# The seam between two matmul layers: loads of w1 and w2 issued ahead of the reload of x1, their conversions and splits moved behind the last tiles' relu

## The chip, the cores and the metric

One core of one Trainium2 chip runs the whole program. The metric is the device time of one execution in microseconds (us), as the median of several runs. TensorE (PE in the profile) does the matmuls, ScalarE (ACT) and VectorE (DVE) the elementwise work on its results, GpSimd (POOL) a part of it, and SyncE (SP) issues the transfers (DMA).

## The reference

A recurrence over time makes `attn_out`; its 3072 tokens of width 384 then go through two feed-forward layers. The seam between those two layers is what this document is about.

```python
def _moe_ref(x, w_in, w_out):            # layer 1: 3072 tokens, 384 -> 2048 -> 384
    h = x @ w_in
    relu6 = np.clip(h + 3.0, 0.0, 6.0)
    g = h * relu6 / 6.0
    return (g @ w_out)

def _moe2_ref(x, w1, w2, w3, w_out):     # layer 2: 384 -> 1024 (twice) -> 1024 -> 384
    a = x @ w1
    b = x @ w2
    h = a * b @ w3
    return (h @ w_out)
```

Everything is in float32 and the matmuls are made precise by splitting: each operand is kept as a high part and a low part, and one product is three matmuls (high by high, high by low, low by high).

## The kernel before

**Layer 1** runs in 6 blocks of 512 tokens (`j`), each in 16 tiles of 128 hidden units (`f`). For one tile `stage_a` does 9 matmuls into a PSUM tile `h` (three chunks of the inner dimension, three matmuls each). `relu_a` (ACT, L435) makes `t`, `evac_a` (DVE, L440) multiplies it with `h`, and `split_g` makes the high part `gh` (ACT, L447) and the low part `gl` (POOL, L451). `stage_b` does 9 matmuls of `gh` and `gl` with the output weights into the three PSUM tiles `acc`. It trails `stage_a` by two tiles (`LAG`), so the last tiles of the last block come on PE as: `h` of tile 14, `acc` of 12, `h` of 15, `acc` of 13, `acc` of 14, `acc` of 15. Then `evac_b` copies `acc` out (ACT, L464), and one DMA for each of the three stores the block to a scratch tensor `x1d` in device memory.

**Layer 2** has 6 blocks of 512 tokens and 8 tiles each. `load_x1` reads a block of `x1d` back into `x1r` (L582), `split_x1` makes `x1h` (ACT, L177) and `x1l` (L178; in block 0 on POOL for the first two of the three parts and on DVE for the third, by `XE`). `stage_c` does 18 matmuls with `x1h` and `x1l` and the weights of one tile (9 for w1 into `h`, 9 for w2 into a tile `wk`), `evac_c` multiplies the two, and `stage_d` multiplies that with the product of w3 and w_out. That product is computed in the kernel, by twelve matmuls at a time between the tiles of the last block of layer 1 (`w34_ticks`: the rows `wk<-wo2h,w3h`).

**The weights** arrive as packed halves and are put together on the chip. For one tile of w1 and w2: `load` issues a DMA of 768 KB into a staging buffer (`stage`, L151; three buffers `st` in turn, and one `stx` for tiles 3 and 7); `conv_a` (ACT, L166) writes `z` from it, into one of two buffers in turn; `conv_d` (DVE, L170) merges `z` into the staging buffer; `split` writes the high part (ACT, L177) and the low part (DVE, L178). The results are `w12ah` and `w12al` for tile 0, `w12h` and `w12l` for the others. `w12_ticks` is a generator that does this for the 8 tiles as a pipeline: tick `t` has `conv_a` of tile `t`, `split` of tile `t-2`, `conv_d` of tile `t-1` and the load of tile `t+2`.

**What sets the order.** There is no scheduler here: each engine takes its instructions in the order in which the code issues them, and waits at an instruction whose operands are not there. SP takes its DMA issues in the same way. Where the ticks stand between the tiles is written in the string `TK`: digit `2f` is the number of ticks of the running generator ahead of `relu_a` of tile `f` in the last block (only up to tile 13, `X1F`), digit `2f+1` the number behind `stage_b` in that step. Behind step 13 the kernel lets `w34_ticks` run out, closes its buffers, issues `load_x1(0)`, and starts `w12_ticks`. The buffer of `x1r` lies where the operands of the w3 product were, so `load_x1(0)` waits for the last of those matmuls.

Of the kernel before, what the change touches and what calls it, by code (L numbers as in the profile page):

```python
# [22 lines left out]
def kernel(  # L23
# [15 lines left out]
    nc = tc.nc  # L39
# [13 lines left out]
    KM = DM // 128  # L53
    KF = wio.shape[1] // (2 * DM)
# [49 lines left out]
    ZC = 2 * DM  # L104
    X1F = 13
    LO = 'w0 k0 r0 w1 k2 r1 w3 k1 n0 n3 r2 w2 k3 n1 r3 n2 s0'
    XE = 'ppv'
    XP = (14, 15, 15)
    XL = 13
    CMIN = 1e-18  # L110

    dram = ctx.enter_context(tc.tile_pool(name="dram", bufs=1, space=DRAM))
# [17 lines left out]
    def pst(tag):  # L130
        return ps.tile([128, 512], F32, tag=tag, name=tag, bufs={"h": 2, "acc": 3, "wk": 3}[tag])
# [7 lines left out]
    wp = wkv.enter_context(tc.tile_pool(name="wk_persist", bufs=1, side="right"))  # L139
    wt = wkv.enter_context(tc.tile_pool(name="wk_t", bufs=1, side="right"))  # L140


    PV = {'p': nc.gpsimd, 'v': nc.vector}

    def bits(ap):
        return ap.bitcast(U32)
# [1 line left out]
    def stage(src, x, n, buf=None):  # L148

        s = st_p.tile([128, 2 * ZC], U32, tag="st", name="st") if buf is None else buf  # L150
        nc.sync.dma_start(out=s[:, 0:2 * n].bitcast(U16), in_=src.bitcast(U16)[:, 4 * x * n + 1:4 * (x + 1) * n + 1])  # L151
        return s[:, 0:2 * n]
# [8 lines left out]
    def conv_a(st):  # L161
        w = st.rearrange("p (n two) -> p n two", two=2)[:, :, 0]
        half = st.bitcast(BF16).rearrange("p (n four) -> p n four", four=4)[:, :, 2]
        z = zs[zn[0] % NZ][:, 0:w.shape[1]]
        zn[0] += 1
        nc.scalar.activation(out=z.bitcast(FP16).rearrange("p (n two) -> p n two", two=2)[:, :, 1], in_=half, func=ACTF.Copy)  # L166
        return w, z

    def conv_d(w, z):
        nc.vector.scalar_tensor_tensor(w, w, 13, bits(z), op0=ALU.logical_shift_right, op1=ALU.bitwise_or)  # L170
        return w.bitcast(F32)
# [4 lines left out]
    def split(raw, hi, lo, lo_eng):  # L176
        nc.scalar.activation(out=hi, in_=raw, func=ACTF.Copy)  # L177
        lo_eng.tensor_tensor(lo, raw, hi.bitcast(F32), op=ALU.subtract)  # L178
# [295 lines left out]

    W0 = 1
    TT = 3
    TK = '11002010110100102302322303011101'
    AH = 4
    ML = 5

# [71 lines left out]
    def f2_open_x():  # L552
        F2.xctx = ExitStack()
        F2.xp = F2.xctx.enter_context(tc.tile_pool(name="x1", bufs=2, side="right", reuse_waits="tile"))

    def w12(f):
        return [t[:, f] for t in F2.w0] if f < W0 else [t[:, f - W0] for t in F2.w]

    def w12_ticks():

        st, zt = {}, {}

        def load(f):
            if f < KF2:
                st[f] = stage(w12d, f, ZC, F2.xp.tile([128, 2 * ZC], U32, tag="stx", name="stx", bufs=1) if f % 4 == 3 else None)

        load(0)
        load(1)
        for t in range(KF2 + 2):
            if t < KF2:  # L570
                zt[t] = conv_a(st[t])
            if t >= 2:
                split(zt.pop(t - 2), *w12(t - 2), nc.vector)
            if 1 <= t < KF2 + 1:
                zt[t - 1] = conv_d(*zt[t - 1])
                st.pop(t - 1)
            load(t + 2)
            yield

    def load_x1(j):  # L580
        s = F2.xp.tile([128, KM, N2], F32, tag="x1r", name="x1r")
        nc.sync.dma_start(out=s, in_=x1d[:, :, j * N2:(j + 1) * N2])  # L582
        F2.x1[j] = [s, F2.xp.tile([128, KM, N2], F32R, tag="x1h", name="x1h"),
                    F2.xp.tile([128, KM, N2], F32R, tag="x1l", name="x1l")]

    def split_x1(j, m):
        s, xh, xl = F2.x1[j]
        split(s[:, m], xh[:, m], xl[:, m], PV[XE[m]] if j == 0 else nc.gpsimd)

    def stage_c(j, f):  # L590
        _, xh, xl = F2.x1[j]
# [216 lines left out]
    if True:  # L808
        make_identity(nc, ident)
        nc.gpsimd.memset(ones, 1.0)  # L810
        for z in zs:
            nc.gpsimd.memset(z, 0.0)
        for x in LO.split()[0:LO1]:
            LD[x[0]](int(x[1]))
        nc.sync.dma_start(out=ubk[0:G], in_=uT)
        nc.scalar.activation(out=ones, in_=ones, func=ACTF.Copy)
        nc.gpsimd.memset(Dp, 0.0)
        nc.gpsimd.memset(Df, 0.0)
        for t in Wb:
            nc.gpsimd.memset(t[0:G, PAD - 1:PAD], 0.0)  # L820
        for t in St:
            nc.gpsimd.memset(t, 0.0)
        for x in LO.split()[LO1:]:
            LD[x[0]](int(x[1]))
        nc.sync.dma_start(out=ubc, in_=u.rearrange("h d -> (h d)").unsqueeze(0).to_broadcast([128, DM]))
        pw = pst("h")

        def warm():
            i16 = ident.bitcast(BF16)
            nc.tensor.matmul(pw[:, 0:256], i16[:, 0:128], i16, start=True, stop=True)  # L830

        wl = w34_ticks()
        units = {}
        nf = dict.fromkeys("GEMHLBV", 0)
        FF = {"G": stage_a, "E": relu_a, "M": evac_a, "H": lambda j, f: split_g(1, j, f, 0),
              "L": lambda j, f: split_g(1, j, f, 1), "B": stage_b, "V": evac_b}
        ONE = {"S": w_load, "O": wio_open, "a": w_a, "d": w_d, "i": w_i, "p": w_p, "D": warm, "w": lambda: next(wl)}

        for x in " ".join(ORDER).split():
            if len(x) > 1:  # L840
                uu = int(x[1:])
                if uu not in units:
                    units[uu] = unit(uu)
                units[uu][x[0]]()
            elif x in nf:
                FF[x](*divmod(nf[x], KM if x == "V" else KF))
                nf[x] += 1
            else:
                ONE[x]()

        steps = [(1, j, f) for j in range(NB) for f in range(KF)] + [(2, j, f) for j in range(NB2) for f in range(KF2)]
        last = NB - 1
        for si in range(last * KF, len(steps) + LAG):
            ph, j, f = steps[si] if si < len(steps) else (3, 0, 0)
            if ph == 1:
                stage_a(j, f)
                if j == last:
                    if f == 0:
                        wkv.close()
                        xt0.close()  # L860
                        w34_open()
                    if f <= X1F:
                        for _ in range(int(TK[2 * f])):
                            next(wl, None)
                relu_a(j, f)
                evac_a(j, f)
                split_g(ph, j, f)
            if ph == 2:
                stage_c(j, f)
                if j == 0:  # L870
                    next(wl, None)
                    split(W34.r[:, f], W34.h[:, f], W34.l[:, f], nc.vector)
                evac_c(j, f)
                split_g(ph, j, f)
            if si >= LAG:
                b = steps[si - LAG]
                if not (ph == 2 and b[0] == 1):
                    (stage_b if b[0] == 1 else stage_d)(*b[1:])
                    if b[0] == 1 and b[2] == KF - 1:
                        for m in range(KM):  # L880
                            evac_b(b[1], m)
            if (ph, j) == (1, last):
                if f == X1F:
                    for _ in wl:
                        pass
                    W34.tctx.close()
                    f2_open_x()
                    load_x1(0)
                    wl = w12_ticks()
                for _ in range(int(TK[2 * f + 1])):  # L890
                    next(wl, None)
                for m in range(KM):
                    if f == XP[m]:
                        split_x1(0, m)
                if f == KF - 1:
                    ph1.close()
                    f2_open_w()
                    for x in range(LAG):
                        stage_b(*steps[si - LAG + 1 + x][1:])
                    for m in range(KM):  # L900
                        evac_b(last, m)
                    next(wl, None)
            if ph == 2:
                if j in (2, 3, 4) and f % 2 == 0:
                    guard_w((j - 2) * 4 + f // 2)
                if (j, f) == (5, 0):
                    guard()
                if f == 1 and j + 1 < NB2:
                    load_x1(j + 1)
                if f in (4, 5, 6) and j + 1 < NB2:  # L910
                    split_x1(j + 1, f - 4)
        man.close()
        F2.xctx.close()
        F2.wctx.close()
        W34.ctx.close()
        main.close()
        okv = nc.values_load(flag, min_val=0, max_val=1)
# [70 lines left out]
```

## Time and profile of the kernel before

| what | value |
|---|---|
| median of 3 runs | 887.28 us (886.37 to 887.92) |
| the profiled execution's own time | 888.7 us |
| its span, first to last instruction | 887.0 us |
| mean granted clock of TensorE | 0.994 of full speed |
| PE busy in the span | 98% |
| ACT, DVE, POOL busy in the span | 37%, 40%, 42% |

A line of the timeline reads: start in us, duration in us, engine, line of the kernel, operation, tile written, tile read, shape, and in square brackets how long the engine was idle before it and what ended that. `acc<-gh,wio2h` is a matmul that writes `acc` with `gh` streaming and a piece of `wio2h` as the stationary weights. A window row has, for each engine, busy us and the number of instructions, then the granted clock of TensorE (1.00 is 2.4 GHz, 0.50 is 1.2 GHz), the busy share of the DMA engines and the GB/s moved. Tile numbers are not in the rows: of the last block, the row order tells them.

### The profile page before, as it was taken

The numbers are of one execution on the slowest core, as the hardware profiler recorded it, in microseconds if no ns is written. First come the engines' busy times: TensorE is split into PE (matmuls) and PEld (weight loads), VectorE is DVE, ScalarE is ACT, GpSimd is POOL, SyncE is SP. The second block draws the span as 40 slices with busy tenths as digits, with TensorE's granted clock in tenths as the row PEclk, the third lists the DMA queues.
The fourth block names the chain that finished last, engine by engine and source line by source line (L and its number), as shares of the span: only waits on it lengthen the run. The fifth ranks groups of instructions, "written<-read, shape, count | busy, mean of one in ns | idle before, by whom it ended". The sixth has DMA issues, their size and how long they took to land.

```text
span 887.0 us, 13899 instructions
## 1 busy us (share of the span) xinstructions
PE 865.2 (98%) x5752; PEld 707.5 (80%) x5752; DVE 357.5 (40%) x537; ACT 330.5 (37%) x556; POOL 375.8 (42%) x337
## 2 busy tenths in 40 slices
PE   7999999999999999999999999899999999999997
PEld 6777677888888888888888888688888888888785
DVE  7799884444444444444213444155111111212110
ACT  1666633333333333343335555365222222222211
POOL 6677877464555555455232211224232222323221
PEclk9999999999999999999999999999999999999999
DMA  9756541212322122221203452560110404030001
GB/s 257 240 193 229 179 123 46 62 62 62 97 62 75 59 86 66 83 81 53 65 1 108 136 176 85 178 212 2 48 45 1 154 1 155 1 133 1 36 1 39
DMA packets 29239, 81.92 MB, mean 92 GB/s; under 512 B 3312, under 2 KB 3440, under 8 KB 29168
## 3 DMA queue, kind: packets, MB, share of 16 engines
q1 hardware_dynamic: 29168, 80.95, 27.9%
q8 instruction: 47, 0.77, 0.3%
q14 instruction: 24, 0.20, 0.1%
HBM read 71.50 MB, written 9.44 MB: 91 GB/s over the span
## 4 chain that ended last, share of the span: by engine, by line
PE 78%; issue 12%; POOL 5%; DVE 3%; ACT 1%; DMA 0%; SPq 0%; POOLq 0%; ACTq 0%; DVEq 0%
PE h L182 9%; PE acc L183 9%; PE acc L182 9%; PE acc L184 9%; PE h L184 9%; PE h L183 9%; PE wk L369 5%; PE wk L183 4%; PE wk L184 4%; PE wk L182 4%; POOL gl L451 4%; PE wk L304 3%; PE wk L348 1%; PE wk L292 1%; POOL A L315 1%
## 5 line engine op out<-in xcount | busy, mean ns | idle before, releaser
L451 POOL TENSOR_TENSOR gl<-t,gh 128x512 fp32r<-128x512 f32 x144 | 192.0, 1334 | 390.6 <-ACT gh L447 390.5
L447 ACT ACTIVATE gh<-t 128x512 fp32r<-128x512 f32 x144 | 91.0, 632 | 193.1 <-DVE t L606 105.9
L440 DVE SCALAR_TENSOR_TENSOR t<-t,h 128x512 f32<-128x512 f32 x96 | 65.3, 681 | 136.2 <-ACT t L435 135.8
L606 DVE TENSOR_TENSOR t<-t,wk 128x512 f32<-128x512 f32 x48 | 33.0, 687 | 202.9 <-PE wk L184 202.9
L435 ACT ACTIVATE t<-h 128x512 f32<-128x512 f32 x96 | 57.3, 597 | 136.8 <-PE h L184 125.1
L182 PE MATMUL h<-xh,wioh 128*128 128x512 f32 x234 | 94.9, 406 | 0.3 <-DVE t L440 0.3
L182 PE MATMUL acc<-gh,wioh 128*128 128x512 f32 x234 | 93.1, 398 | 0.0
L183 PE MATMUL acc<-gl,wioh 128*128 128x512 f32 x234 | 91.6, 392 | 1.0 <-POOL gl L451 1.0
L184 PE MATMUL h<-xh,wiol 128*128 128x512 f32 x234 | 92.2, 394 | 0.3 <-DVE wiol L802 0.3
L183 PE MATMUL h<-xl,wioh 128*128 128x512 f32 x234 | 91.7, 392 | 0.0
L184 PE MATMUL acc<-gh,wiol 128*128 128x512 f32 x234 | 91.4, 391 | 0.0
L605 ACT ACTIVATE t<-h 128x512 f32<-128x512 f32 x48 | 28.6, 596 | 99.6 <-PE h L184 99.6
L183 PE MATMUL acc<-gl,w34h 128*128 128x512 f32 x144 | 56.3, 391 | 0.0
L184 PE MATMUL acc<-gh,w34l 128*128 128x512 f32 x144 | 56.3, 391 | 0.0
L182 PE MATMUL acc<-gh,w34h 128*128 128x512 f32 x144 | 56.2, 390 | 0.0
L182 PEld LDWEIGHTS h<-xh,wioh 128*128 128x128 f32 x234 | 44.0, 188 | 11.7 <-issue 1.3
L184 PEld LDWEIGHTS h<-xh,wiol 128*128 128x128 f32 x234 | 43.9, 188 | 11.1 <-DVE wiol L802 1.3
L183 PEld LDWEIGHTS acc<-gl,wioh 128*128 128x128 f32 x234 | 44.0, 188 | 10.5 <-POOL gl L451 1.6
L184 PEld LDWEIGHTS acc<-gh,wiol 128*128 128x128 f32 x234 | 43.9, 188 | 9.5
L182 PEld LDWEIGHTS acc<-gh,wioh 128*128 128x128 f32 x234 | 44.0, 188 | 9.4 <-issue 0.2
L166 ACT ACTIVATE z<-st 128x768 f16<-128x768 bf16 (+2 forms) x46 | 41.2, 902 | 27.0 <-DVE st L170 8.5
L183 PEld LDWEIGHTS h<-xl,wioh 128*128 128x128 f32 x234 | 44.0, 188 | 8.5
(141 smaller groups left out, 1727.0 us busy)
## 6 DMA issues: line engine op xcount, KB each, us to landing
nat<-in_rkv_dram SPq DMA_DIRECT2D x20, 640.0 KB, 3.9
st<-in_wio_dram SPq DMA_DIRECT2D x16, 768.0 KB, 4.7
st<-in_w3T_dram SPq DMA_DIRECT2D x16, 512.0 KB, 4.4
W<-in_wT_dram SPq DMA_DIRECT2D x24, 224.0 KB, 2.7
K<-in_kT_dram SPq DMA_DIRECT2D x24, 224.0 KB, 2.6
R<-in_rT_dram SPq DMA_DIRECT2D x24, 224.0 KB, 3.0
st<-in_wT_dram SPq DMA_DIRECT2D x12, 448.0 KB, 6.0
x1d<-ev SPq DMA_DIRECT2D x18, 256.0 KB, 2.9
```

The lines of the kernel that those rows point to most:

```text
L166: nc.scalar.activation(out=z.bitcast(FP16).rearrange("p (n two) -> p n two", two=2)[:, :, 1], in_=half, func=ACTF.Copy)
L182: nc.tensor.matmul(ps_ap, lh, rh, start=first, stop=False)
L183: nc.tensor.matmul(ps_ap, lh, rl, start=False, stop=False)
L184: nc.tensor.matmul(ps_ap, ll, rh, start=False, stop=last)
L304: nc.tensor.matmul(d["sc"][h2][:, pr * C:(pr + 1) * C], kh[sl, pr, :], rh[sl, pr, :], start=(pr == 0), stop=(pr == NP - 1), skip_group_che ...
L369: nc.tensor.matmul(px[32 * j:32 * j + 32, m * C:(m + 1) * C], lhs, rhs, start=j not in seen, stop=False, skip_group_check=True)
L435: nc.scalar.activation(out=t, in_=hp[:, 0:N1], func=ACTF.Relu, bias=3.0)
L440: nc.vector.scalar_tensor_tensor(t, t, 6.0, hp[:, 0:N1], op0=ALU.min, op1=ALU.mult)
L447: nc.scalar.activation(out=gh, in_=t, func=ACTF.Copy)
L451: nc.gpsimd.tensor_tensor(gl, t, gh.bitcast(F32), op=ALU.subtract)
L605: nc.scalar.activation(out=a, in_=pp[0][:, 0:N2], func=ACTF.Copy)
L606: nc.vector.tensor_tensor(a, a, pp[1][:, 0:N2], op=ALU.mult)
```

## The change

Four edits, all at the seam:

1. `w12_ticks` issues three loads (tiles 0, 1, 2) at its start instead of two, and stops there once; the loads of the first three tiles are issued ahead of `load_x1(0)` instead of behind it. The number of loads is the same.
2. `TK` holds no tick behind step 13 and two behind step 14: `conv_a` of tiles 0 and 1 now both stand behind relu and split of tile 14.
3. In a tick, `split` of tile `t-2` now stands ahead of `conv_a` of tile `t`.
4. The three parts of `split_x1(0)` are all issued behind step 15, all three low parts on DVE; the tick with `split` of tile 0 and `conv_a` of tile 2 follows them.

```diff
-    XE = 'ppv'
-    XP = (14, 15, 15)
-    XL = 13
...
-    TK = '11002010110100102102322303011101'
+    TK = '11002010110100102302322303000200'
...
-        load(0)
-        load(1)
+        for f in range(3):
+            load(f)
+        yield
         for t in range(KF2 + 2):
+            if t >= 2:
+                split(zt.pop(t - 2), *w12(t - 2), nc.vector)
             if t < KF2:
                 zt[t] = conv_a(st[t])
-            if t >= 2:
-                split(zt.pop(t - 2), *w12(t - 2), nc.vector)
             if 1 <= t < KF2 + 1:
                 zt[t - 1] = conv_d(*zt[t - 1])
                 st.pop(t - 1)
-            load(t + 2)
+            if t >= 1:
+                load(t + 2)
             yield
...
-        split(s[:, m], xh[:, m], xl[:, m], PV[XE[m]] if j == 0 else nc.gpsimd)
+        split(s[:, m], xh[:, m], xl[:, m], nc.vector if j == 0 else nc.gpsimd)
...
                     f2_open_x()
+                    wl = w12_ticks()
+                    next(wl)
                     load_x1(0)
-                    wl = w12_ticks()
                 for _ in range(int(TK[2 * f + 1])):
                     next(wl, None)
-                for m in range(KM):
-                    if f == XP[m]:
+                if f == KF - 1:
+                    for m in range(KM):
                         split_x1(0, m)
-                if f == KF - 1:
+                    next(wl)
                     ph1.close()
                     f2_open_w()
```

On ACT, from the last copy of the w3 product to the first copy of `acc`, before (`t` is the relu of layer 1, the numbers are buffers; `h_5323` and `h_5355` are tiles 14 and 15):

```order
L523 ACTIVATE w34_4550<-wk_5256 128x384
L166 ACTIVATE z0_72<-st_5316 128x768
L435 ACTIVATE t_5333<-h_5323 128x512
L447 ACTIVATE gh_5336<-t_5333 128x512
L166 ACTIVATE z1_73<-st_5318 128x768
L177 ACTIVATE x1h_5314<-x1r_5312 128x512
L435 ACTIVATE t_5365<-h_5355 128x512
L447 ACTIVATE gh_5368<-t_5365 128x512
L166 ACTIVATE z0_72<-st_5321 128x768
L177 ACTIVATE w12ah_4551<-st_5316 128x768
L177 ACTIVATE x1h_5314<-x1r_5312 128x512 x2
L464 ACTIVATE ev_5419<-acc_4647 128x512
```

And in the changed kernel (`h_5322` and `h_5353` are tiles 14 and 15):

```order
L518 ACTIVATE w34_4550<-wk_5256 128x384
L430 ACTIVATE t_5332<-h_5322 128x512
L442 ACTIVATE gh_5335<-t_5332 128x512
L161 ACTIVATE z0_72<-st_5312 128x768
L161 ACTIVATE z1_73<-st_5314 128x768
L430 ACTIVATE t_5363<-h_5353 128x512
L442 ACTIVATE gh_5366<-t_5363 128x512
L172 ACTIVATE x1h_5320<-x1r_5318 128x512 x3
L172 ACTIVATE w12ah_4551<-st_5312 128x768
L161 ACTIVATE z0_72<-st_5316 128x768
L459 ACTIVATE ev_5419<-acc_4647 128x512
```

The conversion of tile 0 moved from ahead of the relu of tile 14 to behind it, and all that touches x1 moved behind the relu of tile 15.

On SP, from the last load of w3 on, before:

```order
L151 DMA st2_5078<-in_w3T_dram 128x2048 [waits DMAHW4_49,DVE_49]
L582 DMA x1r_5312<-x1d_57 128x3x512 [waits PE_49]
L151 DMA st_5316<-in_w12_dram 128x3072 [waits DMAHW3_49]
L151 DMA st_5318<-in_w12_dram 128x3072 [waits DMAHW5_49,DVE_49]
L151 DMA st_5321<-in_w12_dram 128x3072 [waits DMAHW7_49,DVE_49]
L151 DMA stx_5351<-in_w12_dram 128x3072 [waits DVE_49]
```

And in the changed kernel:

```order
L146 DMA st2_5078<-in_w3T_dram 128x2048 [waits DMAHW4_49,DVE_49]
L146 DMA st_5312<-in_w12_dram 128x3072 [waits DMAHW3_49]
L146 DMA st_5314<-in_w12_dram 128x3072 [waits DMAHW5_49,DVE_49]
L146 DMA st_5316<-in_w12_dram 128x3072 [waits DMAHW7_49,DVE_49]
L579 DMA x1r_5318<-x1d_57 128x3x512 [waits PE_49]
L146 DMA stx_5351<-in_w12_dram 128x3072 [waits DVE_49]
```

The issue that waits for PE (`x1r`) stood ahead of the three loads into `st` and now stands behind them.

On DVE, from the evacuation of tile 14 on (`t<-t,h`), before:

```order
L440 SCALAR_TENSOR_TENSOR t_5333<-t_5333,h_5323 128x512
L170 SCALAR_TENSOR_TENSOR st_5316<-st_5316,z0_72 128x768
L440 SCALAR_TENSOR_TENSOR t_5365<-t_5365,h_5355 128x512
L178 TENSOR_TENSOR w12al_4552<-st_5316,w12ah_4551 128x768
L170 SCALAR_TENSOR_TENSOR st_5318<-st_5318,z1_73 128x768
L178 TENSOR_TENSOR x1l_5315<-x1r_5312,x1h_5314 128x512
L178 TENSOR_TENSOR w12l_5400<-st_5318,w12h_5399 128x768
```

And in the changed kernel:

```order
L435 SCALAR_TENSOR_TENSOR t_5332<-t_5332,h_5322 128x512
L165 SCALAR_TENSOR_TENSOR st_5312<-st_5312,z0_72 128x768
L435 SCALAR_TENSOR_TENSOR t_5363<-t_5363,h_5353 128x512
L173 TENSOR_TENSOR x1l_5321<-x1r_5318,x1h_5320 128x512 x3
L173 TENSOR_TENSOR w12al_4552<-st_5312,w12ah_4551 128x768
L165 SCALAR_TENSOR_TENSOR st_5314<-st_5314,z1_73 128x768
L173 TENSOR_TENSOR w12l_5400<-st_5314,w12h_5399 128x768
```

DVE now does all three low parts of x1, ahead of the low part of tile 0's weights; POOL has two subtractions less.

## Rows read from the trace of the kernel before

**Rows 1.** The page's first part: engine, busy us, share of span, instructions.

```profile
PE 865.2 (98%) x5752; PEld 707.5 (80%) x5752; DVE 357.5 (40%) x537; ACT 330.5 (37%) x556; POOL 375.8 (42%) x337
```

**Rows 2.** Timeline of PE, end of layer 1: ends of h 14, h 15, acc 13; then acc 14 and on.

```profile
562.71 0.39 PE L184 MATMUL h<-xh,wio2l 128*128 128x512 f32 x1
...
566.79 0.39 PE L184 MATMUL h<-xh,wio2l 128*128 128x512 f32 x1
...
568.83 0.39 PE L184 MATMUL acc<-gh,wio2l 128*128 128x512 f32 x1
572.82 0.79 PE L182 MATMUL acc<-gh,wio2h 128*128 128x512 f32 x1 [3.61 <-ACT gh L447]
574.18 0.79 PE L183 MATMUL acc<-gl,wio2h 128*128 128x512 f32 x1 [0.57 <-POOL gl L451]
...
580.51 0.39 PE L182 MATMUL h<-x1h,w12ah 128*128 128x512 f32 x1
```

**Rows 3.** Windows of the same stretch, all engines.

```profile
569.10:572.80 3.70, 0.12 (x1) 0.00 (x0) 1.38 (x2) 2.16 (x4) 0.00 (x0) 0.95 1.02 425
572.80:579.00 6.20, 5.61 (x12) 4.09 (x13) 2.03 (x4) 5.28 (x8) 4.47 (x4) 0.50 0.20 84
```

**Rows 4.** Timeline of ACT: relu and gh of tile 13, then from tile 14 on.

```profile
556.98 0.60 ACT L435 ACTIVATE t<-h 128x512 f32<-128x512 f32 x1 [2.85 <-PE h L184]
558.33 0.63 ACT L447 ACTIVATE gh<-t 128x512 fp32r<-128x512 f32 x1 [0.75 <-DVE t L440]
...
569.89 1.06 ACT L166 ACTIVATE z<-st 128x768 f16<-128x768 bf16 x1 [8.33 <-DMA st<-in_w_dram]
570.82 0.57 ACT L435 ACTIVATE t<-h 128x512 f32<-128x512 f32 x1
...
576.91 0.89 ACT L177 ACTIVATE w12ah<-st 128x768 fp32r<-128x768 f32 x1
577.70 1.14 ACT L177 ACTIVATE x1h<-x1r 128x512 fp32r<-128x512 f32 x2
```

**Rows 5.** Windows of PE alone, behind the seam.

```profile
580.51:622.00 41.49, 41.49 (x181) 1.00 0.32 112
```

**Rows 6.** Timeline of SP: the reload of x1, then the loads of w1 and w2.

```profile
561.07 0.63 SPq L582 DMA_DIRECT2D x1r<-x1d  x1
561.75 2.48 SPq L151 DMA_DIRECT2D st<-in_w_dram  x3
```

**Rows 7.** What SP waited for, 530 to 620 us (total, times, longest).

```profile
SPq L582 <- PE wk L184: 18.3, 1, 18.3
```

**Rows 8.** DMA issues 560.5 to 565 us: count, KB each, median us to landing.

```profile
st<-in_w_dram SPq DMA_DIRECT2D x3, 768.0 KB, 8.4
x1r<-x1d SPq DMA_DIRECT2D x1, 768.0 KB, 6.5
stx<-in_w_dram SPq DMA_DIRECT2D x1, 768.0 KB, 11.2
```

**Rows 9.** Timeline of DVE: last low parts of w3, conversion of tile 0.

```profile
550.63 0.69 DVE L178 TENSOR_TENSOR w3l<-st,w3h 128x512 fp32r<-128x512 f32 x1 [0.79 <-ACT w3h L177]
...
553.78 1.33 DVE L178 TENSOR_TENSOR w3l<-st,w3h 128x512 fp32r<-128x512 f32 x1 [1.26 <-ACT w3h L177]
...
572.02 0.95 DVE L170 SCALAR_TENSOR_TENSOR st<-st,z 128x768 uint32<-128x768 uint32 x1
```

**Rows 10.** Timeline of POOL: gl of tiles 12 and 13.

```profile
553.27 1.30 POOL L451 TENSOR_TENSOR gl<-t,gh 128x512 fp32r<-128x512 f32 x1 [7.64 <-ACT gh L447]
559.04 1.29 POOL L451 TENSOR_TENSOR gl<-t,gh 128x512 fp32r<-128x512 f32 x1 [4.47 <-ACT gh L447]
```

**Rows 11.** Windows: a stretch with little DMA, and one with a short wait of PE.

```profile
540.00:560.00 20.00, 19.39 (x98) 17.29 (x98) 8.39 (x12) 9.60 (x17) 3.57 (x3) 1.00 0.09 27
100.00:102.00 2.00, 1.98 (x8) 1.43 (x8) 0.65 (x2) 1.87 (x3) 2.00 (x2) 1.00 1.04 368
```

**Rows 12.** Timeline of PE in that second stretch.

```profile
100.03 0.50 PE L183 MATMUL acc<-gl,wioh 128*128 128x512 f32 x1 [0.97 <-POOL gl L451]
```

More of the change, by code (lines that the diff above doesn't have):

```diff
@@ L140 @@
     wt = wkv.enter_context(tc.tile_pool(name="wk_t", bufs=1, side="right"))
-    PV = {'p': nc.gpsimd, 'v': nc.vector}
     def bits(ap):
@@ L476 @@
     TT = 3
-    TK = '11002010110100102302322303011101'
+    TK = '11002010110100102302322303000200'
     AH = 4
```

## The prediction

> **What bounds the kernel now.** The page's first part comes first: PE is busy for 98% of the span [rows 1], so only a stretch in which PE waits, or runs at a lower clock, can give anything. The list of PE's waits has two of them at the seam and none behind it, which the PE timeline shows in place [rows 2] and a window confirms: from 580.51 to 622 us PE is busy for 41.49 of 41.49 us [rows 5]. At the seam the last matmul of acc of tile 13 starts at 568.83; the first of tile 14 starts at 572.82, after an idle time of 3.61 us that ended with gh; the second waits once more for gl. The windows show what follows: granted clock 0.95 while PE idles and 0.50 (the level of 1.2 GHz) from 572.8 to 579.0 [rows 3].
>
> Next, why gh was late. The matmuls of h of tile 14 end at 562.71 + 0.39 = 563.10 [rows 2], yet its relu starts at 570.82 [rows 4]. Ahead of it in ACT's queue stands the conversion of tile 0 of w1 and w2, which sat from 561.6 to 569.89 waiting for its DMA, 8.33 us [rows 4]. And why that DMA was late: SP waited 18.3 us for the last matmul of the w3 product before it could issue the reload of x1 [rows 7], at 561.07, and the loads stood behind it, from 561.75 on [rows 6]. So a wait of SP for PE made ACT wait, and ACT made PE wait.
>
> **What the seam costs.** Nine matmuls take 568.83 - 566.79 = 2.04 us at full clock [rows 2], 0.227 each. Without waits acc of tile 14 would start at 568.83 + 0.23 = 569.06, and the 18 matmuls of tiles 14 and 15 would end 4.09 us later: layer 2 would start at 573.15. It starts at 580.51 [rows 2]. The seam costs **7.36 us**: 3.76 ahead of the first matmul, 1.13 between first and second (1.36 instead of 0.23), and 2.47 because the other 17 take 6.33 instead of 3.86, at the lower clock.
>
> **Relu of tile 14 (edit 2).** The conversion leaves the place ahead of it. For tile 13 the relu started at 556.98, gh ended at 558.96 and gl at 560.33 [rows 4, 10], so the chain from relu to gl takes 3.35 us and to gh 1.98. By the same lag relu 14 starts near 563.20, gh is there at 565.2 and gl at 566.55, while PE wants them at 569.06: 2.5 us to spare. This removes the 7.36, if nothing new is late.
>
> **Conversions of tiles 0 and 1 (edits 1 and 2).** They now stand between gh 14 and relu 15: two of 1.06 us [rows 4], from 565.1 to 567.2. h 15 ends at 567.18 [rows 2], so they just fit. Then gh 15 is there at 569.3 and gl 15 at 570.6; PE wants gl 15 at 569.06 + 2.04 + 0.23 = 571.33. Spare: 0.7 us. The cover is the h and acc matmuls of tiles 15 and 13; every tenth beyond 0.7 by which the conversions end late would be paid in full.
>
> **The loads (edit 1).** The three loads no longer stand behind the issue that waits for PE; what they wait for is their buffers, the last of which is free when the low part of w3 that starts at 550.63 ends, 551.3 [rows 9]. In the old queue loads took from 8.1 us (the conversion's start, 569.89, less the issue) to 11.2 us to land [rows 4, 6, 8]; even 11.2 would give 562.5, ahead of 565.1. The DMA engines are 9% busy from 540 to 560 [rows 11], so I take nothing for them. The last loads of w3 stand ahead of them in the queue; at most they lose the difference between 8.4 and 6.5, 1.9 us [rows 8], and the last low part of w3 is there at 553.78 + 1.33 = 555.11 [rows 9], 6 us ahead of the end of the product that reads it, 561.07 [rows 6, 7]. Nothing is charged for that either.
>
> **The reload of x1.** Still issued at 561.07, with one transfer behind it instead of four. It took 6.5 us then [rows 8]; 567.6 is ahead of 569.2, when ACT has done gh 15.
>
> **The splits (edits 3 and 4).** On ACT: three high parts of x1 at 0.54 apart (two took 1.14), then w12ah, 0.89 [rows 4]: 569.2 + 1.62 + 0.89 = 571.7, ahead of 573.15. On DVE there is a catch. A subtraction with both inputs in SBUF that started at 553.78, while POOL worked on gl from 553.27 to 554.57, took 1.33 us and ended 0.54 behind POOL's end, where one without POOL beside it took 0.69 [rows 9, 10]. Here the first low part of x1 meets gl 15, which holds until 570.6. So it ends at 571.15, the other two at about 572.4, and w12al, at the 0.95 us that the conversion of as many columns takes [rows 9], at **573.3**. The third matmul of layer 2 is the first that reads w12al, at 573.15 + 0.45 = 573.6, its weight load a matmul earlier, 573.4. It fits by 0.1: I charge 0, with 0.4 as the upper bound.
>
> The Trainium skill (SBUF — State Buffer, Who interferes with whom) says that a VectorE instruction with two SBUF inputs and a GpSimd instruction that reads SBUF exclude each other for the whole instruction, so that the later one blocks fully. The row at 553.78 agrees. By that rule moving work from POOL to DVE gains nothing beside gl 15, which speaks against edit 4; by the sum above it still fits.
>
> **Tile 1 and on.** conv_d of tile 1 ends at 574.2, beside the copies of acc (the last needs the matmuls up to 573.3 and ends near 574.1); w12h of tile 1 at 575.1, w12l at 576.1. PE wants them at 573.15 + 18 x 0.227 = 577.2. Spare 1.1. The load of tile 4 waits for the end of w12al, 573.3; were it as slow as 6.5, it is there at 579.8, and PE wants tile 4 some 14 us later. From there on every engine has the time per tile that it had, and PE had no wait there [rows 5], so all that PE gains at the seam reaches the end.
>
> **Sum.** -7.36 us, between -7.4 and -5.9. The profiled execution took 888.7 with its 887.0 of span, so it would take 881.3 (span 879.6). It lies 1.4 above the median of 887.28; the same taken off the median gives **879.9 us**.
>
> **Rivals.**
> *A small wait stays at the seam.* If conversion 1 ends half a microsecond or a whole one later than I reckon, relu 15, gl 15, then the low parts of x1 (which wait for gl 15) and w12al each slip by that. For it: the spare there is 0.1. Against: the queues ahead are idle, so nothing shows what should delay it. PE would wait 0.4 to 1.5 us. At 100.03 a wait of 0.97 us left the clock at 1.00 [rows 11, 12], so it costs no more than itself: about 880.9.
> *The loads don't run ahead.* If SP got to them only at 561.07, they would take the first places in the queue and x1 the fourth. x1 would land as the fourth did, two microseconds ahead of the fifth's 564.27 + 11.2 = 575.5 [rows 6, 8], at 573.5; its high parts and w12ah end 2.5 us later, 576.0, and PE, having waited about as long as before, pays the 2.47 for the clock: 578.5, a gain of 2.0, 885.3. Against it: in the order the first load carries no wait for PE.
> *x1 late enough to cost more than the old wait.* The mechanism is the fourth place in one queue. Layer 2 starts 2.5 us behind the landing of x1, plus 2.47 for the clock, so the seam is longer than before once x1 lands later than 580.51 - 4.97 = 575.5, where the fifth transfer landed. One more place, 577.5, gives +2.0: 889.3. Against it: only stx is in the queue with it.
> The Trainium skill (DMA: Bandwidth & Descriptors, Queues, rings and completion order) says that each DMA engine takes the descriptors of a ring in order, and the landing times, 6.5 us for the first and 11.2 for the last of five issued within 3.2 us, agree. By that rule x1 now pays for whatever of the three loads is left; by the dates above nothing is left.
> *The change doesn't do what it says,* and ACT still reaches relu 14 behind a wait: 887.3. The order on ACT speaks against it.
>
> **How the numbers follow.** Forecast (gain of 6.9 to 7.5) 0.78; small wait 0.14; loads not ahead 0.03; x1 late 0.02; no effect 0.03. The range runs from the lowest run of before less 7.4, 878.9, to the small wait at its largest (gain 5.9, 881.4) plus the 0.6 by which the highest run lies over the median and a little for the clock: 882.4. A measurement of this kernel can tell about 0.2%, 1.8 us, from no change. The case of the loads not ahead lies on that line and is put down as 0.02 faster and 0.01 not. Faster by more than that: 0.78 + 0.14 + 0.02 = 0.94; within it 0.01 + 0.03 = 0.04; slower 0.02.
>
> **What would show it.** In the changed trace: the first load of tile 0 issued before 552 and x1 still at 561; ACT's relu of tile 14 near 563.2 with no DMA wait ahead of it; PE without an idle row from 554 to 622; layer 2's first matmul near 573.15; a granted clock of 1.00 in every window of the seam; the first low part of x1 on DVE stretched to about 1.4 us by gl 15. Wrong would be: an idle row of PE at acc of tile 15 (conversions late), at the first matmul with x1 (reload late) or with w12al (DVE late), or a clock of 0.50 anywhere behind 560.

## The result, and the profile after

The changed kernel takes 881.01 us, median of 4 runs (878.82 to 881.93), against 887.39 (886.37 to 887.92) for the kernel before beside it: ratio 0.9919, 95% interval 0.9899 to 0.994. A second timing with more runs gave 881.05 (879.56 to 883.16) against 888.45, the same ratio 0.9919, interval 0.9904 to 0.9935. The ratios are not the quotients of the two medians, which are 0.9928 and 0.9917. So the change saves 6.4 us by the first pair of medians, 7.4 by the second, and 7.2 by the ratio; the forecast was 7.4, to 879.9, in a range of 878.9 to 882.4.

The page's first line of the changed kernel (engine, busy us, share of span, instructions; before: [rows 1]):

```profile
PE 860.0 (98%) x5752; PEld 704.2 (80%) x5752; DVE 359.7 (41%) x539; ACT 331.0 (38%) x556; POOL 373.7 (43%) x335
```

PE is busy for 5.2 us less, with the same number of matmuls. Idle time that goes does not show there; matmuls that no longer run at the lower clock do. Of the 5.2, the seam has 3.2 (27.7 us busy before, 24.5 now, between the two ends given below); the rest lies ahead of the seam, and the second trace of the changed kernel does not have it (862.2 in all, 3.0 less). DVE has two instructions more and POOL two less, the low parts of x1. The span is 878.7 us.

The PE timeline of the changed kernel at the seam (first matmuls of acc of tile 14, acc of tile 15, layer 2, and the first that reads w12al; before: [rows 2]):

```profile
568.47 0.39 PE L177 MATMUL acc<-gh,wio2h 128*128 128x512 f32 x1
...
570.51 0.39 PE L177 MATMUL acc<-gh,wio2h 128*128 128x512 f32 x1
...
572.56 0.39 PE L177 MATMUL h<-x1h,w12ah 128*128 128x512 f32 x1
...
573.01 0.39 PE L179 MATMUL h<-x1h,w12al 128*128 128x512 f32 x1
```

No row has a wait in brackets. The same stretch in windows (us, then busy us and count of PE, PEld, DVE, ACT, POOL, the granted clock, DMA share, GB/s; before: [rows 3]):

```profile
560.00:566.00 6.00, 6.00 (x29) 5.00 (x28) 1.08 (x2) 3.13 (x5) 1.30 (x1) 1.00 0.67 186
566.00:572.00 6.00, 6.00 (x28) 4.99 (x27) 4.25 (x6) 5.07 (x9) 1.30 (x1) 1.00 0.19 79
572.00:578.00 6.00, 6.00 (x28) 4.95 (x27) 4.08 (x5) 4.35 (x8) 0.00 (x0) 1.00 0.72 192
```

PE is busy all the time, at 1.00. Where the kernel before had 3.7 us of idle PE and 6.2 us at 0.50, there is nothing left to see.

ACT of the changed kernel (before: [rows 4]):

```profile
562.61 0.60 ACT L430 ACTIVATE t<-h 128x512 f32<-128x512 f32 x1 [1.63 <-PE h L179]
563.97 0.63 ACT L442 ACTIVATE gh<-t 128x512 fp32r<-128x512 f32 x1 [0.75 <-DVE t L435]
564.50 2.02 ACT L161 ACTIVATE z<-st 128x768 f16<-128x768 bf16 x2
566.69 0.60 ACT L430 ACTIVATE t<-h 128x512 f32<-128x512 f32 x1 [0.17 <-PE h L179]
568.04 0.63 ACT L442 ACTIVATE gh<-t 128x512 fp32r<-128x512 f32 x1 [0.75 <-DVE t L435]
568.58 1.66 ACT L172 ACTIVATE x1h<-x1r 128x512 fp32r<-128x512 f32 x3
570.14 0.90 ACT L172 ACTIVATE w12ah<-st 128x768 fp32r<-128x768 f32 x1
```

The relus of tiles 14 and 15 (relu 14 and relu 15 from here on) now wait for PE's own h and for nothing else; the wait of 8.33 us for the DMA is gone. The two conversions fill the place between gh 14 and relu 15 to within 0.17 us.

SP of the changed kernel, the loads and the reload of x1 (before: [rows 6]), and then what the transfers issued from 560 to 562.5 us took to land (before: [rows 8]):

```profile
542.20 8.90 SPq L146 DMA_DIRECT2D st<-in_w_dram  x3
560.48 0.62 SPq L579 DMA_DIRECT2D x1r<-x1d  x1
```

```profile
x1r<-x1d SPq DMA_DIRECT2D x1, 768.0 KB, 6.1
stx<-in_w_dram SPq DMA_DIRECT2D x1, 768.0 KB, 7.3
```

The loads went out between 542.2 and 551.1, each as its buffer came free (SP's waits there are for the low parts of w3 on DVE); the reload of x1 still waits for the w3 product and lands at 566.6, two us ahead of ACT's first use.

DVE and POOL of the changed kernel, around the first low parts of x1 (before: [rows 9, 10]):

```profile
569.23 2.58 DVE L173 TENSOR_TENSOR x1l<-x1r,x1h 128x512 fp32r<-128x512 f32 x3 [1.22 <-ACT x1h L172]
571.73 0.95 DVE L173 TENSOR_TENSOR w12al<-st,w12ah 128x768 fp32r<-128x768 f32 x1
```

```profile
568.75 1.30 POOL L446 TENSOR_TENSOR gl<-t,gh 128x512 fp32r<-128x512 f32 x1 [2.78 <-ACT gh L442]
```

The first of the three subtractions by itself, in a narrower view:

```profile
569.23 1.37 DVE L173 TENSOR_TENSOR x1l<-x1r,x1h 128x512 fp32r<-128x512 f32 x1 [1.22 <-ACT x1h L172]
```

It took 1.37 us, where the two behind it took 0.68 each, and ended 0.55 behind POOL's end at 570.05; all three end at 571.81. The sum had 0.54 for the first behind POOL's end and 0.6 each for the two others. The Trainium skill (SBUF — State Buffer, Who interferes with whom) says that of a VectorE instruction with two SBUF inputs and a GpSimd instruction that reads SBUF the one issued later blocks fully. The trace agrees, with the 0.55 us behind POOL's end. w12al is done at 572.68; its first matmul starts at 573.01.

### The profile page after: what moved, and what is told of

It is laid out like the page before. It is cut to its first block, busy times and chain, and to the rows that moved or that the text cites. A ratio compares the mean times of both kernels' runs of the same rounds, so it can differ in the third digit from the quotient of the medians.

```text
span 878.7 us, 13897 instructions
## 1 busy us (share of the span) xinstructions
PE 860.0 (98%) x5752; PEld 704.2 (80%) x5752; DVE 359.7 (41%) x539; ACT 331.0 (38%) x556; POOL 373.7 (43%) x335
## 5 line engine op out<-in xcount | busy, mean ns | idle before, releaser
L177 PE MATMUL h<-x1h,w12h 128*128 128x512 f32 x126 | 49.9, 396 | 0.0
```

Source lines behind the costliest of these rows:

```text
L177: nc.tensor.matmul(ps_ap, lh, rh, start=first, stop=False)
```

## The experiments

To compare traces, one length is used: the **seam**, from the last copy of the w3 product on ACT (561.07 in the kernel before, 560.49 in the changed one) to the first matmul of layer 2 that reads `w34h` (592.98 and 585.02). What happens ahead of the seam drops out. The early loads run there, so that stretch was compared too: from the wait of PE in the w3 product near 541 to the last copy, the kernel before takes 19.36 us (541.71 to 561.07) and the changed one 19.37 and 19.39 in its two traces. The loads cost nothing there. The kernel before was timed anew beside each group of runs, with medians from 886.6 to 888.5, so ratios are compared here and not microseconds.

| run | seam, us | waits of PE in it | ratio to before (95%) |
|---|---|---|---|
| kernel before | 31.91 | 3.61 and 0.57, clock 0.50 behind | 1 |
| changed, first and second trace | 24.53, 24.54 | none | 0.9919 (0.9904 to 0.9935), second timing |
| edit 1 alone, two traces | 24.55, 24.63 | none | 0.9946 (0.9929 to 0.9963), 0.992 (0.9905 to 0.9935) |
| without edit 1 | 30.05 | 2.54 and 0.84, clock down behind | 0.999 (0.9975 to 1.0004) |
| without edit 4 | 24.60 | none | 0.9927 (0.9911 to 0.9943) |
| without edit 3 | 24.65 | none | one run, 880.88 us |
| changed, relu 15 one conversion later | 25.17 | none in brackets; its weight loads 0.41 and 0.48 | one run, 881.92 us |
| changed, relu 15 three conversions later | 27.39 | 1.06 and 0.85 | 0.9964 (0.9946 to 0.9983) |
| changed, x1 reloaded later | 24.54 | none | one run, 881.63 us |
| edit 1 alone, x1 reloaded later | 26.30 | 0.86 and 0.2 | one run, 883.2 us |
| changed, one tick of w3 moved | 24.53 | none | 0.9944 (0.9931 to 0.9956) |

### The changed kernel again

> The changed kernel as it is, for a narrower interval and a second trace. Theory (the seam alone changed, and nothing behind it gives time back): 7.4 us less than the kernel before, ratio 0.9917, and again no wait of PE from the last w3 product to the end of layer 2. Rival (the first measurement, 6.4 us less, is all there is, since about 1 us is given back elsewhere): ratio 0.993, and a wait or a slower stretch that the kernel before does not have.

The ratio came out as 0.9919, between the two expectations, and nearer to the theory; the seam is 24.54, as in the first trace. Nothing behind the seam waits. From the first matmul that reads `w34h` to the end of the span it is 293.7 us in the first trace (585.02 to 878.7) and 294.0 in the kernel before (592.98 to 887.0). So nothing is given back behind the seam, and the change is worth the seam's 7.38 us; the 6.4 of the first pair of medians lies within the interval of its ratio (5.3 to 9.0 us).

### Edit 1 alone

The kernel before, with this:

```diff
-        load(0)
-        load(1)
+        for f in range(3):
+            load(f)
+        yield
...
-            load(t + 2)
+            if t >= 1:
+                load(t + 2)
...
-                    load_x1(0)
                     wl = w12_ticks()
+                    next(wl)
+                    load_x1(0)
```

> The kernel before with edit 1 alone: the three loads issued ahead of the reload of x1; the conversion of tile 0 still stands ahead of relu 14 and all splits where they were. Theory A (what counts is that SP no longer holds the loads back): the conversion starts at once, near 561.6, relu 14 near 563.2; relu 15 waits for the first high part of x1, which waits for the reload, near 567.6 to 568.2, so gl 15 is about 0.2 us late at most; gain 6.5 to 7.3, 880 to 881. Rival B (what counts is the conversion's place ahead of relu 14 on ACT): relu 14 stays late and the time stays at 886 to 887.

> Edit 1 alone once more, since its first timing (4.8 us less than the kernel before, 3.3 to 6.3) lay below the changed kernel's 7.2 although its trace shows no wait of PE at the seam. Theory (edit 1 alone gives all): 7 us less, ratio 0.992, no wait in the trace. Rival (in other executions the reload of x1 lands later, and relu 15, which here stands behind the first high part of x1, pays for it): again about 5 us less, ratio 0.9945.

The first timing gave 0.9946, the second 0.992; the seam was 24.55 and 24.63, so it was as short as the changed kernel's in both. ACT of this kernel, where the conversion of tile 0 still stands ahead of relu 14:

```profile
559.27 1.08 ACT L166 ACTIVATE z<-st 128x768 f16<-128x768 bf16 x1
561.00 0.60 ACT L435 ACTIVATE t<-h 128x512 f32<-128x512 f32 x1 [0.66 <-PE h L184]
562.36 0.64 ACT L447 ACTIVATE gh<-t 128x512 fp32r<-128x512 f32 x1 [0.76 <-DVE t L440]
562.89 1.09 ACT L166 ACTIVATE z<-st 128x768 f16<-128x768 bf16 x1
564.17 0.63 ACT L177 ACTIVATE x1h<-x1r 128x512 fp32r<-128x512 f32 x1 [0.18 <-DMA x1r<-x1d]
565.08 0.60 ACT L435 ACTIVATE t<-h 128x512 f32<-128x512 f32 x1 [0.28 <-PE h L184]
```

The conversion finds its data there, takes 1.08 us, and is done ahead of relu 14, which waits 0.66 us for PE. Its place in the queue alone never was the fault; the missing data was. Rival B falls: with edit 1 alone the seam is as short as with all four edits, in both traces, and the second timing has the whole gain. The first timing has two thirds of it by its ratio, and why is not settled. The execution that was traced there was the fastest of four, 878.95 us; the other three took 882.52 to 884.44. The second trace shows in small what the rival of the second expectation says:

```profile
563.96 0.63 ACT L177 ACTIVATE x1h<-x1r 128x512 fp32r<-128x512 f32 x1 [0.70 <-DMA x1r<-x1d]
564.50 0.58 ACT L435 ACTIVATE t<-h 128x512 f32<-128x512 f32 x1
```

Here the reload of x1 took 5.8 us to land, against 5.3 in the first trace. ACT waited 0.70 us for it, and relu 15 started 6.33 behind the last copy of the w3 product instead of 6.20; PE had the room for that. In other traces the reload takes up to 6.5 us [rows 8], and a later x1 is tried below. Whether the executions of the first timing that were not traced had such a reload is not shown.

### All edits but the first

The changed kernel, with this:

```diff
-                    wl = w12_ticks()
-                    next(wl)
                     load_x1(0)
+                    wl = w12_ticks()
+                    next(wl)
```

> The changed kernel without edit 1: the reload of x1 again ahead of the three loads, all else as changed. Theory A: relu 14 is on time, but now relu 15 waits behind the conversions of tiles 0 and 1, which wait for DMA until about 569.9 and 571.7; relu 15 near 572.8; PE waits about 3.7 us ahead of acc of tile 15 instead of tile 14, and the clock falls to 0.50 behind it; 886 to 887. Rival B: with relu 14 free most of the gain stays, 880 to 882.

Theory A held: 0.999, not told apart from the kernel before, though one of the ten executions took 882.52 us and the other nine 886.34 to 889.54. ACT, then PE, then two windows:

```profile
564.22 0.60 ACT L430 ACTIVATE t<-h 128x512 f32<-128x512 f32 x1 [1.63 <-PE h L179]
565.58 0.64 ACT L442 ACTIVATE gh<-t 128x512 fp32r<-128x512 f32 x1 [0.75 <-DVE t L435]
570.01 1.08 ACT L161 ACTIVATE z<-st 128x768 f16<-128x768 bf16 x1 [3.79 <-DMA st<-in_w_dram]
571.88 1.06 ACT L161 ACTIVATE z<-st 128x768 f16<-128x768 bf16 x1 [0.79 <-DMA st<-in_w_dram]
572.82 0.57 ACT L430 ACTIVATE t<-h 128x512 f32<-128x512 f32 x1
```

```profile
574.82 0.50 PE L177 MATMUL acc<-gh,wio2h 128*128 128x512 f32 x1 [2.54 <-ACT gh L442]
576.17 0.57 PE L178 MATMUL acc<-gl,wio2h 128*128 128x512 f32 x1 [0.84 <-POOL gl L446]
```

```profile
576.00:578.00 2.00, 1.83 (x5) 1.46 (x6) 2.00 (x4) 2.00 (x4) 0.12 (x1) 0.61 0.00 0
578.00:580.00 2.00, 2.00 (x7) 1.54 (x6) 1.61 (x2) 1.32 (x4) 0.00 (x0) 0.53 0.55 46
```

Relu 14 is on time, and the same DMA wait now holds relu 15: the wait of PE moved by one tile, from acc of 14 to acc of 15, and with it the fall of the clock. The wait was shorter than expected, 2.54 us and not 3.7. Edits 2 to 4, which move the conversions without their data, give 1.86 us of seam (31.91 less 30.05); the end of the timing's interval allows 2.2.

### All edits but the fourth, all but the third

The changed kernel, with the splits of x1 back in their places (and on their engines, by `XE`):

```diff
+    XE = 'ppv'
+    XP = (14, 15, 15)
...
-                if f == KF - 1:
-                    for m in range(KM):
-                        split_x1(0, m)
+                for m in range(KM):
+                    if f == XP[m]:
+                        split_x1(0, m)
+                if f == KF - 1:
                     next(wl)
```

> The changed kernel without edit 4: the three parts of x1 split where and on the engines where they were before (one behind step 14, two behind step 15; POOL, POOL, DVE). Theory: the first high part waits for the reload until about 567 and makes relu 15 0.3 to 0.9 us late, and its low part stands ahead of gl 15 on POOL; gl 15 has 0.7 to spare, so PE waits 0 to 0.5 us and the time is that of the changed kernel, 880 to 881.5. Rival (moving x1 behind relu 15 and off POOL is a large part of the gain): a wait of PE of 1.5 us or more, with the clock down behind it, 883 or more.

The seam is 24.60, 0.07 longer, without a wait of PE, and the ratio 0.9927. The first high part of x1 stood ahead of relu 15 (it starts 6.44 us behind the last copy of the w3 product instead of 6.20), and the room at gl 15 took that in.

The changed kernel, with the conversion ahead of the split again:

```diff
+            if t < KF2:
+                zt[t] = conv_a(st[t])
             if t >= 2:
                 split(zt.pop(t - 2), *w12(t - 2), nc.vector)
-            if t < KF2:
-                zt[t] = conv_a(st[t])
```

> The changed kernel without edit 3: in a tick the conversion again ahead of the split, so the conversion of tile 2 stands ahead of w12ah on ACT. Theory: w12ah ends one conversion later, 0.93 us, at about 0.6 ahead of its first use, and w12al 0.2 later than in the changed kernel, which had 0.1 to spare: PE waits 0 to 0.3 us; 881. Rival (edit 3 is what makes the weights arrive in time): a wait of 1 us or more at the first matmuls of layer 2.

Seam 24.65, 0.1 longer. DVE took up w12al 0.26 later, 11.50 behind the last copy of the w3 product instead of 11.24, with a wait for w12ah in it:

```profile
572.40 0.96 DVE L173 TENSOR_TENSOR w12al<-st,w12ah 128x768 fp32r<-128x768 f32 x1 [0.18 <-ACT w12ah L172]
```

Edits 3 and 4 are each worth a tenth of a microsecond here at most; the two traces of edit 1 alone differ by 0.08.

### How much room there is

The changed kernel, with the conversion of tile 1 repeated once or (`range(3)`) three times, so that relu 15 comes later:

```diff
                 zt[t] = conv_a(st[t])
+                for _ in range(1 if t == 1 else 0):
+                    zn[0] -= 1
+                    zt[t] = conv_a(st[t])
```

> The changed kernel with the conversion of tile 1 done twice, so that relu 15 comes one conversion later (0.93 us, of which ACT idled 0.17 there). Theory (spare of 0.7 us at gl 15, of 0.1 at w12al, every tenth beyond is paid): relu 15 slips by 0.76; gl 15 just about in time, w12al 0.65 late; PE waits 0.6 to 0.8 us in all, mainly at the third matmul of layer 2, clock 1.00 throughout. Rival (there is more spare than the trace shows, since the queues absorb it): no wait of PE.

> The same with three extra conversions: relu 15 slips by 2.6 us. Theory: PE waits 1.9 us at acc of tile 15 (0.8 for gh, the rest for gl) and 0.6 more for w12al, 2.5 us in all; if the clock stays up, 2.5 us more than the changed kernel, 883.5; if the waits take it down as the 3.6 us of the kernel before did, up to 2.5 more, 886. Rival (more spare): under 1.5 us of waits.

One extra conversion lengthens the seam by 0.64 us, three by 2.86. The weight loads of PE show where, for one extra conversion:

```profile
571.30 0.19 PEld L178 LDWEIGHTS acc<-gl,wio2h 128*128 128x128 f32 x1 [0.41 <-POOL gl L446]
...
573.92 0.19 PEld L179 LDWEIGHTS h<-x1h,w12al 128*128 128x128 f32 x1 [0.48 <-DVE w12al L173]
```

And PE and two windows for three:

```profile
571.18 0.50 PE L177 MATMUL acc<-gh,wio2h 128*128 128x512 f32 x1 [1.06 <-ACT gh L442]
572.53 0.50 PE L178 MATMUL acc<-gl,wio2h 128*128 128x512 f32 x1 [0.85 <-POOL gl L446]
```

```profile
570.50:572.50 2.00, 0.50 (x1) 0.19 (x1) 0.82 (x1) 2.00 (x4) 1.27 (x1) 1.00 0.00 0
572.50:574.50 2.00, 1.97 (x9) 1.63 (x10) 2.00 (x4) 2.00 (x4) 0.00 (x0) 1.00 0.00 0
```

And DVE's w12al for one and for three:

```profile
572.92 0.95 DVE L173 TENSOR_TENSOR w12al<-st,w12ah 128x768 fp32r<-128x768 f32 x1
574.15 0.95 DVE L173 TENSOR_TENSOR w12al<-st,w12ah 128x768 fp32r<-128x768 f32 x1
```

Relu 15 came 0.81 and 3.03 us later than in the changed kernel, counted from the last copy of the w3 product, and w12al 0.78 and 2.97. Of the latter 0.64 and 2.86 were lost, so the room at w12al is 0.1 us, as expected, and what goes beyond it is paid in full.

The places were not all as expected: with one extra conversion PE waited nearly as much for gl 15 as for w12al, where it was to be mainly w12al, and with three the loss was 2.86 and not 2.5. The room at gl 15 is about 0.4 us and not 0.7: in the changed trace gl 15 ends at 570.05 and the weight load of its first matmul starts at 570.51; with relu 15 coming 0.81 later that load waited 0.41.

With three extra conversions, between the two waits, PE was busy for 0.50 of 2.00 us, and the granted clock stayed at 1.00, unlike behind the waits of 2.54 and 0.84 above. The two waits of 1.06 and 0.85 made layer 2 start 2.46 us later: a wait in brackets counts from the end of the matmul before it, which in steady flow reaches 0.16 us into the next, and the matmul behind each wait started 0.34 us on instead of 0.23.

The timing with three conversions, 0.9964, is 3.2 us better than before, where the changed kernel is 7.2 better: 4.0, each with an interval of about 1.5 to either side, against 2.86 in the trace.

### What edit 4 is good for

Both the changed kernel and edit 1 alone, with the load into stx ahead of the reload of x1:

```diff
-        for f in range(3):
+        for f in range(4):
             load(f)
...
-            if t >= 1:
+            if t >= 2:
                 load(t + 2)
```

> The changed kernel with the load into stx (768 KB, tile 3) issued ahead of the reload of x1 instead of behind it, so that x1 lands about 2 us later. Theory (edit 4 takes the reload of x1 off relu 15's path): relu 15 is not touched; x1 lands near 568, before or as ACT gets to its first high part; seam as in the changed kernel or up to 0.5 us longer, no wait of PE at acc of tile 15. Rival (the order of the splits makes no difference): the same wait here as in the run with edit 1 alone and x1 later.

> Edit 1 alone with the load into stx issued ahead of the reload of x1. Theory: here relu 15 stands behind the first high part of x1, so it comes about as much later as x1 lands later, 1.5 to 2 us, and with the 0.7 to spare PE waits 0.8 to 1.5 us at acc of tile 15; seam 1 to 2 us longer than with edit 1 alone, clock 1.00. Rival (the order of the splits makes no difference): seam as in the changed kernel with x1 later.

ACT of the changed kernel with x1 later, relu 15 and the high parts of x1:

```profile
567.77 0.60 ACT L430 ACTIVATE t<-h 128x512 f32<-128x512 f32 x1 [0.17 <-PE h L179]
569.12 0.63 ACT L442 ACTIVATE gh<-t 128x512 fp32r<-128x512 f32 x1 [0.75 <-DVE t L435]
569.66 1.66 ACT L172 ACTIVATE x1h<-x1r 128x512 fp32r<-128x512 f32 x3
```

And of edit 1 alone with x1 later, ACT and then PE:

```profile
568.85 0.63 ACT L177 ACTIVATE x1h<-x1r 128x512 fp32r<-128x512 f32 x1 [2.35 <-DMA x1r<-x1d]
569.39 0.58 ACT L435 ACTIVATE t<-h 128x512 f32<-128x512 f32 x1
```

```profile
572.77 0.50 PE L183 MATMUL acc<-gl,wio2h 128*128 128x512 f32 x1 [0.86 <-POOL gl L451]
```

Both reloads took about 7 us. In the changed kernel no wait came of it: seam 24.54, with x1 there at 569.2, 0.4 us ahead of ACT's first use. With the splits in their old places relu 15 stood behind a DMA wait of 2.35 us, and the seam grew to 26.30, 1.7 more. The two runs differ in edits 2 and 3 too, and each was traced once; that it is edit 4 is read from ACT's rows, where x1's first high part stands ahead of relu 15. So edit 4 saves next to nothing as long as x1 is early, and takes a second wait of the same kind out of reach.

### A tick of the w3 pipeline moved

```diff
-    TK = '11002010110100102302322303000200'
+    TK = '11002010110100102302322204000200'
```

One tick went from behind step 11 to behind step 12; the rest is the changed kernel.

> The changed kernel with one tick of the w3 pipeline moved from behind step 11 to behind step 12 (TK), to take away the wait of 0.4 to 1.2 us that PE has near 541, where a conversion waits for its load of w3. Theory: the load gets one step more, that wait goes, the seam keeps its 24.5 us; 0.5 to 1 us less than the changed kernel in the trace, hardly to be seen in the timing: ratio 0.991. Rival: the wait moves to another tick and the time stays, ratio 0.992.

The rival held: the conversion still waited, PE had waits of 0.47 and 0.35 us in the w3 pipeline in place of one of 0.43 to 1.23 in the two traces of the changed kernel, and the ratio of 0.9944 is no better than the changed kernel's. It is even about 2 us worse, the intervals just meeting; the trace does not show why, since the seam stayed at 24.53. No run here beat the changed kernel by more than the scatter.

## Why the prediction was right, and where it was not

- **What the seam costs.** 7.36 forecast, 7.38 found (31.91 less 24.53).
- **The dates.** The changed trace reaches the end of h 14 at 562.51 (a matmul start of 562.12 and 0.39), 0.59 ahead of the kernel before. Less that 0.59, and with the prediction's own lags from h to relu and from relu to gl, the forecast had relu 14 at 562.61 (found 562.61), relu 15 at 566.69 (566.69), the end of gl 15 at 570.04 (570.05), of w12al at 572.7 (572.68), and layer 2 at 572.56 (572.56). The working from row to row held to a few hundredths, because each term was a duration that stood in a row and each start the later of two ends.
- **The block between DVE and POOL** was in the sum with its size and left 0.1 us of room at w12al. The runs with later conversions show that this was the room: 0.64 and 2.86 us lost for a w12al that came 0.78 and 2.97 later. The 0.7 at gl 15 was too large. It was reckoned to the start of the matmul, where the working for w12al went by the weight load one matmul earlier; the run with one extra conversion shows about 0.4. It did not bear on the time, since w12al had less.
- **The bound of 0 for the early loads** held: 4.9 us to land, median, and from the wait near 541, which the kernel before has too, to the last copy of the w3 product PE takes as long as before (19.37 against 19.36).
- **What was credited to the wrong edit.** The working said that moving the conversion away from relu 14 (edit 2) removes the 7.36. It does not: with edits 3 and 4, but without edit 1, it moved the wait to the next tile and kept all but 1.86 us of it, and edit 1 without edit 2 gave the whole gain in the seam. The chain in the prediction's first part (SP waits for PE, ACT for the DMA, PE for ACT) had named the right cause; the costing then took the last link for it. The sum was right since both edits were in the change; a forecast for edit 2 without edit 1, made by that line of the working, would have been wrong.
- **The rival of loads that don't run ahead** was priced at a gain of 2.0. The run without edit 1, which makes just that happen, had 1.86 in the seam. In detail it went otherwise: x1 landed first and the conversions held relu 15, where the rival had x1 fourth.
- **The median** is 1.1 us above the forecast. The seam is not short of it, and the scatter is larger than it. By its size the first gain, 6.4 us, falls into what the prediction gave to a small wait at the seam (5.9 to 6.9). There was none in either trace, so the number alone would have named the wrong case.
- **What a small wait costs** was put at no more than itself. The waits of 1.06 and 0.85 us cost 2.46, about 0.28 more than each one's length, with the clock at 1.00.

## What to carry to other kernels

When an engine waits at an instruction for a DMA, look first at what the DMA's issue waited for: a load whose buffer is free should not stand in the issuing queue behind one that waits for a matmul. Moving the waiting instruction back in its own queue without its data moved the wait to the next tile here. To size such an edit, add up the stretch from row to row to the next instruction that would be late, and then delay it on purpose: the cost for each delay tells how much room there is.

## What the runs showed that was not expected

- **The clock and the waits.** Waits of PE of 1.06 and 0.85 us, 0.5 us of work between them, left the granted clock at 1.00; 2.54 and 0.84 took it to 0.61 and 0.53 in the next two windows of 2 us; 3.61 and 0.57 to 0.50 [rows 2, 3], which cost 2.47 us on top of the waits. But the length of a wait does not settle what the clock does. Every trace has a wait of PE of 3.6 to 4.1 us near 8 us. In the kernel before, PE's row and a window behind it (busy us and count of PE, granted clock, DMA share, GB/s):

```profile
8.32 1.87 PE L325 MATMUL acc<-ubk,q 112*128 112x2 f32 x8 [3.71 <-POOL q L319]
8.00:13.00 5.00, 4.68 (x28) 1.00 1.06 270
```

And with edit 1 alone, first trace:

```profile
8.40 1.87 PE L325 MATMUL acc<-ubk,q 112*128 112x2 f32 x8 [3.80 <-POOL q L319]
8.00:13.00 5.00, 4.60 (x28) 0.50 1.05 257
```

Of the 13 traces, four show the lower clock there (waits of 3.73 to 4.09 us) and nine do not (3.62 to 3.87). So the 2.47 us stand for the execution that was traced; whether the clock falls at the seam in every execution of the kernel before is not shown, and their mean granted clock goes from 0.988 to 0.997 in the second timing.

- **Scatter from the first 140 us.** The first store of a block of layer 1 starts at 142.5 us in the kernel before, at 141.2 and 142.6 in the two traces of the changed kernel, and at 139.9 and 140.2 in those of edit 1 alone, though up to there the order of the work is the same. These differences run through to the end, and they are as large as what a timing can tell. The four traces with the lower clock near 8 us have it at 139.9 to 141.6, the nine others at 140.95 to 142.8. What makes these differences was not tried.
